# Moving the one-pass matmul operands of a two-branch kernel to the low part of SBUF

## The chip, the core and the metric

The kernel runs on one core of a Trainium2 chip. The metric is the time of one execution on the device in microseconds: the median of several runs of the kernel. Beside the timed runs there is one profiled execution, from which the span (first to last instruction) and every trace row come.

## The reference

Two independent branches are computed, and their results stand side by side in the output of 2048 rows and 2048 columns.

```python
# branch A: attention with 32 query heads of width 32 and one shared key/value head
q = (x @ wq).reshape(B, S, H, Dh)          # S = 2048, D = 1024, H = 32, Dh = 32
k = x @ wk; v = x @ wv
p = softmax(einsum("bhqd,bkd->bhqk", q, k) * Dh ** -0.5)
a = einsum("bhqk,bkd->bhqd", p, v).reshape(B, S, H * Dh) @ wo
# branch B: real part of a Fourier transform along the hidden and the sequence axis
re = einsum("bsd,ed->bse", xb, dft_hid_re); im = einsum("bsd,ed->bse", xb, dft_hid_im)
y = einsum("ts,bse->bte", dft_seq_re, re) - einsum("ts,bse->bte", dft_seq_im, im)
out = concatenate([a, y], axis=-1)
```

All inputs are float32.

## The kernel before, in words

**Precision.** A float32 matmul in full precision shows in the trace as two matmul records. A matmul whose two operands are of type float32r shows as one, here called a one-pass matmul. A float32 value is split into a rounded part and a remainder (names ending in h and l, "hi" and "lo"), and a product of full accuracy is made of three one-pass matmuls, hi·hi, hi·lo and lo·hi (`product`, line 373). The scores also use one-pass matmuls: key and query are stacked on the partition axis as (kh, kh, kl) against (qh, ql, qh), so that one pass makes the three terms. The attention weights times v (`pv`, line 821) use full float32.

**Streams of work.** TensorE carries two interleaved streams.

- The attention goes by 32 units of one block of 512 queries and one group of four heads. Each unit has 32 steps. `scores(s)` (line 744) makes two one-pass matmuls into a PSUM tile `pss` with moving operand `kst` and weights from `qst`; VectorE takes a negated maximum from it, and ScalarE an exponential and its sum (`row_sums`), out of which come the softmax constants. `expo(n)` (line 807), 44 steps behind, makes the transposed scores: two one-pass matmuls into `pst` with moving operand `qst` and weights from `kst`, and ScalarE writes their exponential to `p`. Three times in a unit `pv` multiplies `p` with `v` in full float32, four heads at a time. 
- Everything else is a queue of groups: the projection of the queries, the products of the Fourier branch and of the output projection (block recursions with seven products for eight). Each group adds up products of a left item (weights, tiles `mh` and `ml`) and a right item (moving operand, tiles `rh` and `rl`) into a PSUM tile `psb`. `take(n)` (line 379) issues n of these matmuls; `level` (line 933) spreads them over the steps of the attention, so that a step has about five. In a step in which `pv` runs, `level` issues none.

The order on each engine is the order of the program: every instruction goes through a wrapper that keeps it (line 79 is the line of that wrapper, and so the line that every instruction shows in the profile).

**How the items come.** For both lines of items (`Line`, line 154) SyncE loads raw blocks to staging tiles (`r0`, `r1` for the right, `m0`, `m1` for the left), GpSimd adds or subtracts them where a recursion asks for it, rounds them to `rh` or `mh` and writes the remainder to `rl` or `ml` (`hi_r`, `hi_m`, `lo`). 14 buffers of `rh` and of `rl` and four of `mh` and of `ml` go round.

**The end.** After the last unit the last eight groups run without scores between them. Their last right item meets the newest attention output, tiles `oh` and `ol`, as weights (`last_block`, line 364), while the moving operand is `rh` or `rl`.

**Where the tiles lie.** SBUF tiles come from pools. A pool takes its place when it is opened, from the left (low addresses upwards) by default, or from the right (high addresses downwards) with `side="right"`. Before the change:

- from the left, in this order: `keep` (`kst`, `v`, the identity), `qsp` (three tiles of `qst`, 8 KB in a partition each), `pp` (13 tiles of `p`, 4 KB each), `sm` (maxima, sums and the softmax constants), `onp` (`rb`, `ov`, `oh`, `ol`, 2 KB each);
- from the right, in this order: `r0p` and `m0p` (staging, five tiles of 2 KB each), `rp` (28 tiles of 2 KB), `mp` (8 tiles of 2 KB), `yp` (6 tiles of 2 KB), `op` (3 tiles of 2 KB).

The two stacks together nearly fill the partition. All pools live as long as the kernel, so no two of them ever share a place. At the start, before `p`, `rb` and the staging tiles have their own use, they hold the blocks of the attention input.

Of the kernel before, what the change touches and what calls it, by code (L numbers as in the profile page):

```python
# [101 lines left out]
def tile_kernel(ctx: ExitStack, tc, xT, wq, wkv, wo, xbT, wT, cT, out):  # L102
# [8 lines left out]
    def pool(stack, name, bufs, **kw):  # L111
        kw.setdefault("reuse_waits", "tile")
        return stack.enter_context(tc.tile_pool(name=name, bufs=bufs, **kw))
# [28 lines left out]
    NR, NM = 14, 4  # L142
    r0p = pool(ctx, "r0p", NR0, side="right")
    m0p = pool(ctx, "m0p", NM0, side="right")
    rp = pool(ctx, "rp", NR, side="right")
    mp = pool(ctx, "mp", NM, side="right")
    yp = pool(ctx, "yp", NY, side="right")
    op = pool(ctx, "op", 3, side="right")

# [566 lines left out]
    qsp = pool(ctx, "qsp", 1)  # L716
    rows = []
    NP = 13
    pp = pool(ctx, "pp", NP)
    sm = pool(ctx, "sm", 2)  # L720
    onp = pool(ctx, "onp", 1)

    units = [(b, g) for b in range(NQ) for g in range(NG)]
    SU = 32
# [308 lines left out]
```

## Time and profile before

| | |
|---|---|
| runs (three) | 2742.67 us median, 2741.53 to 2744.46 |
| profiled execution, span | 2740.7 us; no time around the span is recorded for it |
| TensorE (PE) busy | 2733.4 us, 13820 matmuls |
| weight loads (PEld) busy | 1917.8 us, 13820 |
| VectorE (DVE) busy | 1596.6 us |
| ScalarE (ACT) busy | 2159.8 us |
| GpSimd (POOL) busy | 1721.8 us |
| TensorE clock granted | 1.000 of full speed on average |

A row of the groups reads: line, engine, operation, out<-in by tile names, shapes, xcount, then busy time in us and the mean length of one in ns, then the idle time of the engine before them and what ended it. In `MATMUL psb<-rh,mh`, the first name behind the arrow is the moving operand and the second the weights. A row of the timeline begins with the start and the length in us; rows of one kind behind each other are merged, with their count at the end (x2). Matmul lengths overlap the next matmul and their ends are modelled, so the time that one takes of TensorE is read from one start to the next.

### The profile page before, as it was taken

To read this page: it belongs to the slowest core of one execution; us is meant where nothing else is said; L and a number is where in the kernel's file an instruction comes from. 1 tells how busy PE (TensorE), PEld (TensorE's weight loads), DVE (VectorE), ACT (ScalarE), POOL (GpSimd) and SP (SyncE) were. 2 spreads that over 40 slices of the span, in tenths; PEclk is the share of its full clock that TensorE was granted. 3 is DMA by queue.
4 is the path that set the end of the run, shared out by engine and by line. 5 is a ranking of instruction groups with operands and counts; after the bars stand their busy time and mean duration, and the time that the engine had idled before them with its cause. 6 is when DMAs were issued, how large, how long until landed. Compare 5 with 4: busy or idle time off the path is not lost.

```text
span 2740.7 us, 40561 instructions
## 1 busy us (share of the span) xinstructions
PE 2733.4 (100%) x13820; PEld 1917.8 (70%) x13820; DVE 1596.6 (58%) x1826; ACT 2159.8 (79%) x3131; POOL 1721.8 (63%) x1711
## 2 busy tenths in 40 slices
PE   9999999999999999999999999999999999999999
PEld 6876767667676767667676776667676676767667
DVE  5766666666676666555565556666555555655411
ACT  3588878888887888888888888888888888888741
POOL 4854425777647558765556665576787887865751
PEclk9999999999999999999999999999999999999999
DMA  8643336887777666564354688874675765644565
GB/s 273 191 136 120 117 96 205 281 270 232 248 261 271 202 219 187 168 203 136 125 158 149 184 251 285 290 253 124 209 222 158 219 192 160 206 137 136 185 208 188
DMA packets 316931, 538.24 MB, mean 196 GB/s; under 512 B 35962, under 2 KB 63354, under 8 KB 316666
## 3 DMA queue, kind: packets, MB, share of 16 engines
q1 hardware_dynamic: 315572, 533.69, 61.6%
q8 instruction: 109, 1.79, 0.3%
q10 hardware_dynamic: 1152, 1.97, 0.2%
q14 instruction: 98, 0.80, 0.1%
HBM read 395.58 MB, written 138.15 MB: 195 GB/s over the span
## 4 chain that ended last, share of the span: by engine, by line
PE 98%; DMA 1%; SPq 0%; issue 0%; POOL 0%; ACT 0%; DVE 0%; DVEq 0%; POOLq 0%; ACTq 0%
PE psb L79 61%; PE pss L79 19%; PE pst L79 18%; DMA y<-u 0%; SPq L79 0%; DMA y<-c 0%; DMA qh<-in_wo_dram 0%; DMA rb<-r 0%; DMA m<-in_wq_dram 0%; POOL rl L79 0%; ACT p L79 0%; DVE y L79 0%; POOL ml L79 0%; DVE nm L79 0%; POOL m L79 0%
## 5 line engine op out<-in xcount | busy, mean ns | idle before, releaser
L79 DVE TENSOR_REDUCE nm<-pss 128x1 f32<-128x1024 f32 x1024 | 1252.8, 1224 | 572.5 <-PE pss L79 571.0
L79 ACT ACTIVATE p<-pst 128x1024 f32<-128x1024 f32 x1026 | 1056.0, 1029 | 449.7 <-PE pst L79 445.9
L79 ACT ACTIVATE pss<-pss,nm 128x1024 f32<-128x1024 f32 x1024 | 1116.0, 1090 | 61.3 <-DVE nm L79 59.2
L79 PE MATMUL psb<-rh,mh 128*128 128x512 f32 x1790 | 705.4, 394 | 1.0 <-DVE y L79 0.9
L79 PE MATMUL psb<-rh,ml 128*128 128x512 f32 x1790 | 704.2, 393 | 0.0
L79 PE MATMUL psb<-rl,mh 128*128 128x512 f32 x1790 | 704.0, 393 | 0.0
L79 PE MATMUL pss<-kst,qst 128*128 128x512 f32 x2048 | 653.7, 400 | 0.3
L79 PE MATMUL pst<-qst,kst 128*128 128x512 f32 x2048 | 650.3, 398 | 0.8 <-ACT p L79 0.7
L79 POOL TENSOR_TENSOR ml<-m,mh 128x512 fp32r<-128x512 f32 x366 | 471.8, 1289 | 35.8 <-ACT mh L79 26.5
L79 PEld LDWEIGHTS pss<-kst,qst 128*128 128x128 f32 x2048 | 374.6, 188 | 160.9 <-issue 76.3
L79 PE MATMUL psb<-p,v 128*32 128x512 f32 x4096 | 459.3, 594 | 0.0
L79 PEld LDWEIGHTS pst<-qst,kst 128*128 128x128 f32 x2048 | 374.9, 188 | 110.1 <-ACT p L79 26.1
L79 PEld LDWEIGHTS psb<-rh,mh 128*128 128x128 f32 x1790 | 336.2, 188 | 85.7 <-issue 2.4
L79 PEld LDWEIGHTS psb<-rl,mh 128*128 128x128 f32 x1790 | 336.1, 188 | 79.8 <-DVE rl L79 1.2
L79 PEld LDWEIGHTS psb<-rh,ml 128*128 128x128 f32 x1790 | 336.2, 188 | 79.0
L79 POOL CAST mh<-m 128x512 fp32r<-128x512 f32 x365 | 223.0, 611 | 245.9 <-PE psb L79 218.7
L79 PEld LDWEIGHTS psb<-p,v 128*32 128x32 f32 x4096 | 123.3, 110 | 283.7 <-issue 275.8
L79 POOL TENSOR_TENSOR m<-m,m 128x512 f32<-128x512 f32 x220 | 283.4, 1288 | 58.1 <-DMA m<-o 23.2
L79 POOL TENSOR_TENSOR rl<-r,rh 128x512 fp32r<-128x512 f32 x208 | 268.2, 1290 | 4.0
L79 POOL CAST rh<-r 128x512 fp32r<-128x512 f32 x208 | 127.5, 613 | 199.9 <-PE psb L79 149.6
L79 ACT ACTIVATION_READ_ACCUMULATOR pss<-pss,nm 128x1 f32 x1024 | 212.5, 207 | 0.0
L79 POOL TENSOR_TENSOR r<-r,r 128x512 f32<-128x512 f32 x120 | 154.8, 1290 | 72.8 <-DMA r<-in_wT_dram 44.8
(92 smaller groups left out, 790.5 us busy)
## 6 DMA issues: line engine op xcount, KB each, us to landing
m<-in_cT_dram SPq DMA_DIRECT2D x384, 256.0 KB
r<-s SPq DMA_DIRECT2D x192, 256.0 KB
y<-y SPq DMA_DIRECT2D x128, 256.0 KB
r<-in_wT_dram SPq DMA_DIRECT2D x88, 256.0 KB
m<-in_xbT_dram SPq DMA_DIRECT2D x88, 256.0 KB
y<-u SPq DMA_DIRECT2D x80, 256.0 KB
m<-in_wq_dram SPq DMA_DIRECT2D x64, 256.0 KB
qst<-qh SPq DMA_DIRECT2D x64, 256.0 KB
```

Source lines behind the costliest of these rows:

```text
L79: return lambda *a, **k: self.tc.keep_in_program_order(f(*a, **k))
```

## The change

Five pools change sides. `rp` and `mp`, which hold the operands of the products, move from the right to the left stack and come to lie right above `keep`, below `qsp`. `pp`, `sm` and `onp` move from the left to the right stack, below `op`. The pools keep their sizes and the number of their buffers, and everything else of the kernel is as before.

```diff
     r0p = pool(ctx, "r0p", NR0, side="right")
     m0p = pool(ctx, "m0p", NM0, side="right")
-    rp = pool(ctx, "rp", NR, side="right")
-    mp = pool(ctx, "mp", NM, side="right")
+    rp = pool(ctx, "rp", NR)
+    mp = pool(ctx, "mp", NM)
     yp = pool(ctx, "yp", NY, side="right")
     op = pool(ctx, "op", 3, side="right")
...
     qsp = pool(ctx, "qsp", 1)
     rows = []
     NP = 13
-    pp = pool(ctx, "pp", NP)
-    sm = pool(ctx, "sm", 2)
-    onp = pool(ctx, "onp", 1)
+    pp = pool(ctx, "pp", NP, side="right")
+    sm = pool(ctx, "sm", 2, side="right")
+    onp = pool(ctx, "onp", 1, side="right")
```

## The prediction

> **What bounds the kernel now.** I read the page from the top first: busy shares, the clock, then the chain that ended last.
>
> ```profile
> span 2740.7 us, 40561 instructions
> PE 2733.4 (100%) x13820; PEld 1917.8 (70%) x13820; DVE 1596.6 (58%) x1826; ACT 2159.8 (79%) x3131; POOL 1721.8 (63%) x1711
> PEclk9999999999999999999999999999999999999999
> PE 98%; DMA 1%; SPq 0%; issue 0%; POOL 0%; ACT 0%; DVE 0%; DVEq 0%; POOLq 0%; ACTq 0%
> ```
>
> TensorE is busy for 2733.4 of 2740.7 us at full clock, and 98% of the chain is TensorE. Only the time between the starts of two matmuls can move the end. The groups by form tell how many there are, and which other engine is nearest.
>
> ```profile
> L79 PE MATMUL psb<-rh,mh 128*128 128x512 f32 x1790 | 705.4, 394 | 1.0 <-DVE y L79 0.9 <-ACT rh L79 0.2
> L79 PE MATMUL pss<-kst,qst 128*128 128x512 f32 x2048 | 653.7, 400 | 0.3
> L79 PE MATMUL pst<-qst,kst 128*128 128x512 f32 x2048 | 650.3, 398 | 0.8 <-ACT p L79 0.7
> L79 PE MATMUL psb<-p,v 128*32 128x512 f32 x4096 | 459.3, 594 | 0.0
> L79 PEld LDWEIGHTS pst<-qst,kst 128*128 128x128 f32 x2048 | 374.9, 188 | 110.1 <-ACT p L79 26.1 <-issue 3.4
> ```
>
> The 400 ns are a modelled length with overlap; what counts is start to start. One-pass matmuls are three times 1790 products, 2048 + 2048 of the scores, and some 150 in other PSUM tiles at the end: about 9620. So I went to the timeline of TensorE: one step of the main loop, and the starts of the steps behind it.
>
> ```profile
> 1500.21 0.63 PE L79 MATMUL pss<-kst,qst 128*128 128x512 f32 x2
> 1500.68 0.63 PE L79 MATMUL pst<-qst,kst 128*128 128x512 f32 x2
> 1501.15 0.40 PE L79 MATMUL psb<-rh,mh 128*128 128x512 f32 x1
> 1501.38 0.39 PE L79 MATMUL psb<-rl,mh 128*128 128x512 f32 x1
> ...
> 1502.06 0.40 PE L79 MATMUL psb<-rl,mh 128*128 128x512 f32 x1
> 1502.30 0.63 PE L79 MATMUL pss<-kst,qst 128*128 128x512 f32 x2
> ...
> 2458.72 0.62 PE L79 MATMUL pst<-qst,kst 128*128 128x512 f32 x2
> ...
> 2481.67 0.62 PE L79 MATMUL pst<-qst,kst 128*128 128x512 f32 x2
> ```
>
> A step is two score matmuls, two of the transposed scores and five products: nine in 2.09 us. Between the last two rows lie eleven such steps: 22.95 us, 2.086 a step, 0.2318 a matmul. Now the end of the kernel, where products run alone and then meet the weights of the last unit (oh, ol).
>
> ```profile
> 2711.95 0.40 PE L79 MATMUL psb<-rh,ml 128*128 128x512 f32 x1
> 2712.18 0.39 PE L79 MATMUL pss<-rh,oh 128*128 128x512 f32 x1
> 2712.41 0.39 PE L79 MATMUL pss<-rl,oh 128*128 128x512 f32 x1
> ...
> 2714.74 0.40 PE L79 MATMUL psb<-rh,ol 128*128 128x512 f32 x1
> 2714.98 0.39 PE L79 MATMUL psb<-rh,mh 128*128 128x512 f32 x1
> 2715.21 0.39 PE L79 MATMUL psb<-rl,mh 128*128 128x512 f32 x1
> 2715.43 0.39 PE L79 MATMUL psb<-rh,ml 128*128 128x512 f32 x1
> ...
> 2719.06 0.39 PE L79 MATMUL psb<-rh,mh 128*128 128x512 f32 x1
> ```
>
> From 2715.43 to 2719.06 lie sixteen products: 3.63 us, 0.2267 each, the settled pitch. The twelve with oh or ol as weights take 2.80 us, 0.2333 each. Their moving operands are still rh and rl; only the place of the weights is another, and the next products settle again within two or three.
>
> The places follow from the pools. Counted in bytes within a partition, the left pools hold kst from 17,024, qst from 27,264 to 51,839, p to 105,087, oh and ol from 111,872 to 115,967. The right ones hold mh from 135,136, ml to 151,519, rh and rl from 151,520 to 208,863. So products read both operands high, scores read both low, and the oh matmuls read weights low and moving data high. Within the high part the place doesn't matter: the sixteen settled products walk through several of the 28 buffers of rh and rl and several columns of mh and ml. My reading: a matmul whose weights and moving data lie in different parts is late, and it takes some matmuls to settle afterwards. A loop step crosses twice, from products to scores and back. It takes 2.086 us where nine settled ones would take 9 x 0.2267 = 2.040: 46 ns more.
>
> **The change part by part.** No instruction is added, removed or reordered, no wait changes, and every DMA has its size and queue. Only addresses change. Summing the pool sizes in the new order, rh and rl come to 27,264 to 84,607, mh and ml to 100,991, qst to 125,567; kst stays. p, the sums and exponentials go high with the staging, oh and ol to about 130,400.
>
> *One-pass matmuls.* All operands of a loop step then lie in one stretch, below 125,568, as the products' did before within 73,700 bytes. I take the settled pitch for all nine. There are 1024 steps (2048 pst matmuls by two). 96 of them hold the p,v matmuls (three for each of 32 units) and no product, so they don't cross; some 31 hold a transpose that upsets the pitch anyway, for which I take half. The other 1024 - 96 - 31 = 897 x 46 ns give 41.3 us, and 31 x 23 ns give 0.7. The prologue has 44 score steps of two score matmuls and seven products:
>
> ```profile
> 92.89 0.62 PE L79 MATMUL pss<-kst,qst 128*128 128x512 f32 x2
> 94.98 0.62 PE L79 MATMUL pss<-kst,qst 128*128 128x512 f32 x2
> ```
>
> Nine in 2.09 us here too: 44 x 46 ns = 2.0 us. Bounds: nothing from below (the pitch of the low part by itself is never seen settled, since runs there are four long); from above everything that TensorE takes beyond 9620 x 0.2267 = 2181 us. Its busy time less 459.3 of p,v and some 23 of other full-precision matmuls and transposes is 2251, so 70 us; the part beyond 44 is starts after the p,v blocks and waits, which no address removes.
>
> *p,v matmuls* now read p high and v low, a crossing. The nearest rows are the full-precision matmuls that make k and v, whose weights lie low (ov, 110 kB up) and whose moving data alternate:
>
> ```profile
> 28.55 0.59 PE L79 MATMUL pss<-p,ov 128*64 128x512 f32 x1
> 28.56 0.59 PE L79 MATMUL pss<-r,ov 128*64 128x512 f32 x1
> 28.98 0.59 PE L79 MATMUL pss<-p,ov 128*64 128x512 f32 x1
> 29.41 0.59 PE L79 MATMUL pss<-p,ov 128*64 128x512 f32 x1
> ```
>
> p lies low, r high, and each pair takes 0.43 us whichever comes first. I take 0; at the other end 7 ns (0.2333 less 0.2267) on each of the 1024 groups of four, 7 us.
>
> *Other engines.* POOL multiplies low tiles and combines high ones in the same time:
>
> ```profile
> L79 POOL TENSOR_TENSOR r<-r,r 128x512 f32<-128x512 f32 x120 | 154.8, 1290 | 72.8 <-DMA r<-in_wT_dram 44.8 <-DMA r<-s 12.7 <-DMA s<-y 12.2
> L79 POOL TENSOR_TENSOR oh<-ov,rb 128x512 f32<-128x512 f32 x16 | 20.7, 1293 | 112.9 <-DVE ov L79 109.3 <-DMA ql<-y 3.6
> ```
>
> 1290 against 1293 ns: place costs it nothing, and I take the same for DVE and ACT, with 63, 58 and 79% busy as cover.
>
> *What is late next.* ACT. Where it is behind, its cycle from p to p is 1.99 us:
>
> ```profile
> 1379.05 1.03 ACT L79 ACTIVATE p<-pst 128x1024 f32<-128x1024 f32 x1
> 1381.04 1.04 ACT L79 ACTIVATE p<-pst 128x1024 f32<-128x1024 f32 x1
> ```
>
> A step of nine at 2.04 still covers that, by 0.05 instead of 0.10. A step of eight does not, and where they come every other step TensorE already waits for p:
>
> ```profile
> 238.72 0.63 PE L79 MATMUL pst<-qst,kst 128*128 128x512 f32 x2
> ...
> 1380.32 0.62 PE L79 MATMUL pst<-qst,kst 128*128 128x512 f32 x2
> 1382.18 0.68 PE L79 MATMUL pst<-qst,kst 128*128 128x512 f32 x2
> 1384.32 0.62 PE L79 MATMUL pst<-qst,kst 128*128 128x512 f32 x2
> ...
> 2679.04 0.39 PE L79 MATMUL pst<-qst,kst 128*128 128x512 f32 x1
> ```
>
> Eight from 1380.32 to 1382.18 (1.86 us), then nine in 2.14: together 4.00, ACT's pace. Such pairs gain nothing. Waits of this kind add up to 26.1 us before the weight loads of pst, most of it hidden by the matmul ahead. Of the plain steps I count 89 of eight (the first starts at 238.72, the last at 2679.04), so with their partners some 178, and put 130 of them at ACT's pace: 130 x 46 ns = 6.0 us lost (0 if the slack that TensorE has on ACT after each p,v block covers them, 8.2 if all are caught).
>
> The sum: 41.3 + 0.7 + 2.0 - 6.0 = 38.0 us less. The profiled span of 2740.7 becomes 2702.7; the median of the runs, 2742.67, lies 2.0 us above that span, so the time is 2704.7.
>
> One rule speaks against all this. The Trainium skill, "SBUF — State Buffer", section "Who interferes with whom", gives TensorE two read ports, one for the moving operand and one for the weights, independent of each other, says that it never waits on anyone, and makes nothing depend on the place within a partition. By that rule the time stays 2742.7; the twelve matmuls at 0.2333 beside the sixteen at 0.2267 disagree with it, and they are all that disagrees.
>
> **The rivals.**
> *Nothing moves (2742.7).* The late pitch could come from something else that the scores and the oh matmuls share and the settled products lack: a change of the tile pair by itself, or the semaphores that free pss and pst. For it: the scores among themselves, all low, don't run settled (1500.21 to 1501.15 is 0.235 each), although they share one part. Against it: four are too few to settle, and PSUM banks change at the end of the kernel too, between products, at the settled pitch.
>
> *Slower.* The cost may belong to weights read from the low part, whatever the moving data. For it: all low weights that are seen, of scores and of oh, run at 0.233 to 0.235. Against it: the products behind the crossing, whose weights are high, start late too (1501.15 to 1501.38 is 0.23). Then each of the nine takes 0.2333, a step 2.100 us, 14 ns more than 2.086, on 941 steps 13 us, and some 400 products outside such steps 2.6 us more: 2742.7 + 16 = 2759. It decides from the point where the settled pitch of the low part is over 0.232.
>
> *Half.* The part that counts may end inside the new block (between rl and qst, say), as no trace shows a pair across 52,000 to 110,000. Then about one crossing of two stays: half of 38.0, about 2724.
>
> Whether it is the part, or the 32 bytes by which right-hand tiles stand off a multiple of 64 while left-hand ones don't, the trace can't tell; the change makes both alike, so the sum is the same.
>
> **How the numbers follow.** Like operands settle: 0.64, and its own range is 2697 to 2714 (all 44 us of steps and no loss to ACT give 2699; p,v matmuls that do feel the crossing and ACT's full loss give 2714; 2 us for the runs' spread at the lower end). Half: 0.09. Nothing: 0.15. Slower: 0.12. A change of 0.2%, 5.5 us, is about what can be told from none here. The first two are faster (0.73), the third the same, the fourth slower. The range runs from 2692 to 2746: it takes in nothing-moves with the spread of the runs and leaves out the slower case and little else.
>
> **What would show it.** Right: a nine-matmul step of 2.04 us from pss to pss, ten in 2.27, the score matmuls at 0.227 among products, and the p,v groups unchanged; ACT's busy time the same with a larger share, and more idle time behind ACT p in the weight loads of pst. The prologue's step falls alike, with no ACT p in it. Wrong: a step still at 2.09 (the cause is in the pair or the semaphores), one at 2.10 or more (low weights), or steps at 2.04 with a span that doesn't follow, which would mean new waits on ACT, POOL or the loads that feed rh and mh.

## The result and the profile after

The changed kernel takes 2709.98 us (median, 2709.76 to 2710.24) against 2742.1 us in the same runs: the ratio is 0.988, with a 95% interval of 0.9866 to 0.9894. The profiled execution has a span of 2708.2 us in a time of 2709.95; it was 32.5 us longer before. The granted clock of TensorE is 1.0 in both. The forecast was 2704.7.

From the page of the changed kernel, the rows that answer to those of before:

```profile
span 2708.2 us, 40561 instructions
PE 2700.9 (100%) x13820; PEld 1917.0 (71%) x13820; DVE 1595.7 (59%) x1826; ACT 2135.1 (79%) x3131; POOL 1721.4 (64%) x1711
PE 99%; DMA 0%; ACT 0%; DVE 0%; POOL 0%; issue 0%; SPq 0%; ACTq 0%; DVEq 0%; POOLq 0%
```

The instructions are the same in number. The busy time of TensorE fell by 32.5 us, the whole difference of the spans; VectorE and GpSimd are unchanged within 1 us. ScalarE's busy time fell by 24.7 us, although the mean lengths of its three large groups are the same within 2 ns (1091 after 1090, 1031 after 1030, 209 after 207): its records overlap more, they did not get shorter. From the groups by form:

```profile
L79 PE MATMUL psb<-p,v 128*32 128x512 f32 x4096 | 459.3, 594 | 0.0
L79 PEld LDWEIGHTS pst<-qst,kst 128*128 128x128 f32 x2048 | 373.5, 188 | 107.4 <-ACT p L79 30.8 <-issue 3.4
```

The p,v matmuls take 459.3 us as before. The waits for ACT's p grew from 26.1 to 30.8 us. The timeline of TensorE, one step of nine in the main loop, and two starts of the prologue:

```profile
92.12 0.61 PE L79 MATMUL pss<-kst,qst 128*128 128x512 f32 x2
94.16 0.61 PE L79 MATMUL pss<-kst,qst 128*128 128x512 f32 x2
...
2442.15 0.62 PE L79 MATMUL pss<-kst,qst 128*128 128x512 f32 x2
2442.60 0.61 PE L79 MATMUL pst<-qst,kst 128*128 128x512 f32 x2
...
2444.19 0.39 PE L79 MATMUL pss<-kst,qst 128*128 128x512 f32 x1
```

Nine matmuls take 2.04 us in both places, 0.2267 each, where they took 2.09. Two score matmuls now take 0.45 us instead of 0.47. So the gain came where the forecast put it. Why it came had still to be found out, since two readings gave the same number: the part of the partition, and the offset of the tiles.

### The profile page after: what moved, and what is told of

It reads as the page before. It is cut to its first block, busy times and chain, and to the rows that moved or that the text cites. A ratio compares the mean times of both kernels' runs of the same rounds, so it can differ in the third digit from the quotient of the medians.

```text
span 2708.2 us, 40561 instructions
## 1 busy us (share of the span) xinstructions
PE 2700.9 (100%) x13820; PEld 1917.0 (71%) x13820; DVE 1595.7 (59%) x1826; ACT 2135.1 (79%) x3131; POOL 1721.4 (64%) x1711
## 4 chain that ended last, share of the span: by engine, by line
PE 99%; DMA 0%; ACT 0%; DVE 0%; POOL 0%; issue 0%; SPq 0%; ACTq 0%; DVEq 0%; POOLq 0%
PE psb L79 62%; PE pss L79 19%; PE pst L79 18%; DMA y<-c 0%; ACT pss L79 0%; DVE nm L79 0%; DMA rb<-r 0%; DMA m<-in_wq_dram 0%; SPq L79 0%; ACT p L79 0%; DVE y L79 0%; POOL ml L79 0%; POOL m L79 0%; DVE qh L79 0%; ACT mh L79 0%
## 5 line engine op out<-in xcount | busy, mean ns | idle before, releaser
L79 ACT ACTIVATE p<-pst 128x1024 f32<-128x1024 f32 x1026 | 1056.3, 1030 | 443.6 <-PE pst L79 432.1
L79 ACT ACTIVATE pss<-pss,nm 128x1024 f32<-128x1024 f32 x1024 | 1117.3, 1091 | 59.5 <-DVE nm L79 56.9
L79 PE MATMUL pss<-kst,qst 128*128 128x512 f32 x2048 | 645.3, 396 | 0.3
L79 PE MATMUL pst<-qst,kst 128*128 128x512 f32 x2048 | 642.9, 395 | 0.6 <-ACT p L79 0.4
L79 PE MATMUL psb<-p,v 128*32 128x512 f32 x4096 | 459.3, 594 | 0.0
L79 PEld LDWEIGHTS pst<-qst,kst 128*128 128x128 f32 x2048 | 373.5, 188 | 107.4 <-ACT p L79 30.8
```

The costliest lines, as they stand in the source:

```text
L79: return lambda *a, **k: self.tc.keep_in_program_order(f(*a, **k))
```

## The experiments

The theory on record was that of the part: late where weights and moving data lie on different sides of a border. Its rivals were the offset of tiles against each other, and weights read from the low part being slow in themselves.

**A map of places.** A kernel of its own, with nothing at work but TensorE:

```diff
+    def run(m, mo, w, wo_):
+        o = ps[n[0] % 2]
+        n[0] += 1
+        for _ in range(REP):
+            te.matmul(o, s[w][:, wo_:wo_ + P], s[m][:, mo:mo + W], start=True, stop=True)
```

> This kernel leaves the whole computation out: it fills SBUF with 25 tiles of 8 KB a partition (sa at 16,512 to sy at 213,120, all on multiples of 64 bytes) and runs blocks of 40 one-pass matmuls, 128x512, with the weights in one tile and the moving data in another, no other engine at work. First weights in sc (32,896), moving data in each tile in turn; then weights in su (180,352); then the same with the moving data fixed and the weights going round; then one pair with its moving data shifted by 4 to 400 bytes; then weights in steps of 512 bytes across 131,072. Theory of the part: 0.2267 us per matmul where both lie on one side of a border between 115,968 and 135,136, and about 0.233 where they lie on different sides, in both directions; no effect of the shifts. Theory of the 32 bytes: 0.2267 for all pairs of tiles, about 0.233 where the moving data are shifted by 32 bytes. Theory of low weights: 0.233 for all blocks with weights in the low tiles, 0.2267 for all with high ones, wherever the moving data lie.

Timeline of this kernel; each row is a block of 40 (`REP`) matmuls of the same pair, and the time to the next block's start over 40 is the pitch. Moving tile and weights tile stand behind the arrow (one name where they are the same tile).

```profile
34.11 9.23 PE L31 MATMUL pb<-sd,sc 128*128 128x512 f32 x40
43.17 9.23 PE L31 MATMUL pa<-se,sc 128*128 128x512 f32 x40
...
188.24 9.23 PE L31 MATMUL pa<-su,sc 128*128 128x512 f32 x40
197.31 9.23 PE L31 MATMUL pb<-sv,sc 128*128 128x512 f32 x40
...
251.71 9.23 PE L31 MATMUL pb<-sc,su 128*128 128x512 f32 x40
260.77 9.23 PE L31 MATMUL pa<-sd,su 128*128 128x512 f32 x40
...
922.64 9.62 PE L31 MATMUL pb<-sc 128*128 128x512 f32 x40
932.11 9.49 PE L31 MATMUL pa<-sc 128*128 128x512 f32 x40
...
950.70 9.49 PE L31 MATMUL pa<-sc 128*128 128x512 f32 x40
960.03 9.31 PE L31 MATMUL pb<-sc 128*128 128x512 f32 x40
...
1134.66 9.47 PE L31 MATMUL pa<-sc,sn 128*128 128x512 f32 x40
1143.96 9.26 PE L31 MATMUL pb<-sc,so 128*128 128x512 f32 x40
```

Weights low and moving data low (34.11 to 43.17) take 9.06 us; weights low and moving data at 180,352 (188.24) take 9.07; weights at 180,352 and moving data low (251.71) take 9.06: 0.2267 a matmul each, but for the rounding of the rows. Of the 100 blocks of the four sweeps 99 read like these; the first, at the very start of the kernel, takes 10.78 us. So the theory of the part fell, and that of low weights with it. A moving operand shifted by 4 bytes takes 0.2368 (922.64 to 932.11), by 32 bytes 0.2333 (950.70 to 960.03). The last pair belongs to the steps towards 131,072: there the weights were moved by 128 bytes modulo 256, still below that address, and took 0.2325, while the steps of 2,048 and 512 bytes before it were settled, and so was the tile above after its first matmuls. That block told that the offset modulo 256 was the thing to vary.

**32 bytes of padding, all operands low (e2).** The changed kernel with a pad of 32 bytes below the product tiles and one above:

```diff
+    off_a = pool(ctx, "off_a", 1).tile([P, 8], F32, name="off_a")
     rp = pool(ctx, "rp", NR)
     mp = pool(ctx, "mp", NM)
+    off_b = pool(ctx, "off_b", 1).tile([P, 8], F32, name="off_b")
+    gp.memset(off_a, 0.0)
+    gp.memset(off_b, 0.0)
```

> The changed kernel with rh, rl, mh and ml 32 bytes further up, so that they stand 32 bytes off a multiple of 64 as before the change, while kst and qst stand on multiples of 64 as before; all of them stay low. Theory of the part: 2710 us as changed, steps of nine at 2.04. Theory of the 32 bytes: the crossings are back, steps of nine at 2.086, about 2742.

2741.84 us; ratio to the kernel before 0.9999 (0.9989 to 1.0008). The whole gain is gone with every operand still low. From its timeline, eleven steps of nine:

```profile
2461.22 0.63 PE L79 MATMUL pst<-qst,kst 128*128 128x512 f32 x2
...
2484.21 0.63 PE L79 MATMUL pst<-qst,kst 128*128 128x512 f32 x2
```

22.99 us, 2.090 a step. It does not show 32 bytes by itself, though: the second pad put qst at 192 modulo 256 bytes, with kst at 128 and the products at 160, so that the scores were a mismatched pair too.

**Weights of the products high again (e3).**

```diff
-    mp = pool(ctx, "mp", NM)
+    mp = pool(ctx, "mp", NM, side="right")
```

> The changed kernel with mh and ml back in the high part (192,480 to 208,863), rh and rl low, kst and qst low. Every product then reads weights high and moving data low, the scores both low. Theory of the part: the products never settle, five at 0.233 and four score matmuls that don't settle among them, a step of nine at 2.09 to 2.10, and the products alone at the end at 0.233 too: 2745 to 2760 us, slower than the changed kernel and no faster than the kernel before. Theory of low weights: products at 0.2267, since their weights are high, scores late: 2720 to 2745.

2744.47 us, 1.0007 of before (0.9997 to 1.0016): as the theory of the part had it but for half a microsecond below its range. It agrees with the offset as well, since mh and ml came to 224 modulo 256 and rh and rl stayed at 128. The products alone at its end:

```profile
2703.22 0.40 PE L79 MATMUL pst<-rh,mh 128*128 128x512 f32 x1
...
2708.14 0.40 PE L79 MATMUL psb<-rh,mh 128*128 128x512 f32 x1
```

From the first of these rows to the last lie 21 products, 4.92 us, 0.2343 each: a mismatched pair stays late for good. This run could not tell the two theories apart; the map did.

**A map of offsets.**

> This kernel too leaves the whole computation out; it runs blocks of 40 one-pass matmuls, and only the offset of the moving data to the weights changes. Section a: moving data 0, 16, 32 up to 256 bytes further up, one tile after the other (sa to sq). Section b: weights 32 to 256 bytes further up (sr to sy). Section c: both further up by 4, 8, 16, 32, 64, 96 and 128 bytes. Sections d and e: five matmuls of one pair and four of another in turn, the second pair further up by 96 bytes in d and by 256 in e. Theory of the relative offset (the settled pitch holds where moving data and weights stand at the same place modulo 256 bytes): in a and b 0.2267 at 0 and 256 bytes alone and 0.229 to 0.237 between; all of c at 0.2267; d at about 0.2318, as in the loop of the kernel before, and e at 0.2267. Theory of the absolute place (tiles have to stand on a multiple of 64 or 128 bytes): c late at 4 to 32 bytes, d settled or nearly so.

```profile
24.05 9.50 PE L31 MATMUL pa<-sc 128*128 128x512 f32 x40
33.39 9.49 PE L31 MATMUL pa<-sd 128*128 128x512 f32 x40
42.72 9.33 PE L31 MATMUL pa<-se 128*128 128x512 f32 x40
51.88 9.41 PE L31 MATMUL pa<-sf 128*128 128x512 f32 x40
...
144.99 9.24 PE L31 MATMUL pa<-sp 128*128 128x512 f32 x40
154.06 9.28 PE L31 MATMUL pa<-sq 128*128 128x512 f32 x40
163.17 9.49 PE L31 MATMUL pb<-sr 128*128 128x512 f32 x40
...
209.81 9.33 PE L31 MATMUL pb<-sw 128*128 128x512 f32 x40
218.99 9.49 PE L31 MATMUL pb<-sx 128*128 128x512 f32 x40
...
228.31 9.24 PE L31 MATMUL pb<-sy 128*128 128x512 f32 x40
237.39 9.66 PE L31 MATMUL pc<-sa 128*128 128x512 f32 x40
246.89 9.40 PE L31 MATMUL pc<-sb 128*128 128x512 f32 x40
256.13 9.48 PE L31 MATMUL pc<-sc 128*128 128x512 f32 x40
265.45 9.28 PE L31 MATMUL pc<-sd 128*128 128x512 f32 x40
274.56 9.26 PE L31 MATMUL pc<-se 128*128 128x512 f32 x40
...
301.86 1.30 PE L31 MATMUL pd<-sa 128*128 128x512 f32 x5
303.00 1.10 PE L31 MATMUL pd<-sb 128*128 128x512 f32 x4
303.94 1.31 PE L31 MATMUL pd<-sa 128*128 128x512 f32 x5
...
347.58 1.30 PE L31 MATMUL pe<-sa 128*128 128x512 f32 x5
...
349.62 1.30 PE L31 MATMUL pe<-sa 128*128 128x512 f32 x5
```

Moving data 32 bytes up (sc, 24.05) take 0.2335, 64 bytes (se) 0.2290, 256 bytes (sq) 0.2267 but for the first matmuls of the block. Weights 256 bytes up (sy) are settled, weights 32 bytes up (sr) are not, and weights 192 bytes up (sw), which is 64 short of 256, take 0.2295, about as much as moving data 64 bytes up: it is the place of the one against the other, modulo 256. Four blocks don't fit that theory. Moving data 240 bytes up, 16 short of 256, are settled as well (sp, 144.99 to 154.06). And the pair that is shifted together settles by 32 bytes and more (sd, 265.45 to 274.56, but for its first matmuls), but not by 4, 8 or 16 bytes (sa, sb and sc of section c: 0.2375, 0.2310 and 0.2330). So in these blocks a match was enough only where both started on a multiple of 32. Section d is the loop of the kernel before in small: five of one pair and four of another 96 bytes off take 2.08 us (301.86 to 303.94), where the loop took 2.086. In section e, 256 bytes off, nine took 2.04 (347.58 to 349.62), although the pair of tiles changes just as often.

**The kernel before, aligned (e5).** All pools on their old sides, and 96 bytes above the right-hand stack:

```diff
+    off = pool(ctx, "off", 1, side="right").tile([P, 24], F32, name="off")
+    gp.memset(off, 0.0)
     r0p = pool(ctx, "r0p", NR0, side="right")
```

> The kernel before with every pool where it was, and 96 bytes left free above the right-hand stack, so that rh, rl, mh and ml stand at 128 modulo 256 bytes as kst and qst do, products still high and scores low. Theory of the relative offset: the whole gain without moving a pool, steps of nine at 2.04, 2710 us within 2. Theory of the part: nothing, 2742.

2710.77 us, 0.9883 of before (0.9868 to 0.9897): the whole gain, with products high and scores low.

```profile
1501.88 0.61 PE L79 MATMUL pss<-kst,qst 128*128 128x512 f32 x2
1503.92 0.61 PE L79 MATMUL pss<-kst,qst 128*128 128x512 f32 x2
```

The step of nine is 2.04 us. This run decides it: that the operands came to lie low did nothing.

**The step between the pairs alone, and 256 bytes.** As in e2, but with qst moved by 256 bytes (e6); and rh, rl, mh, ml and qst all moved by 256 (e7).

> The changed kernel with rh, rl, mh and ml 32 bytes further up and qst 256, so that the pairs within the products and within the scores keep the same place modulo 256 bytes and only the step between the two kinds is off by 32. Theory of the relative offset: two crossings a step as before the change, steps of nine at 2.08 to 2.09, 2735 to 2745 us. If crossings cost nothing and only pairs count: 2710.

> The changed kernel with rh, rl, mh, ml and qst 256 bytes further up, and nothing else. Theory of the relative offset modulo 256 bytes: as the changed kernel, 2710 us within 2. If the place of the one-pass operands to each other counts in bytes and not modulo 256: late, over 2720.

e6 takes 2733.26 us (ratio 0.9964, 0.9951 to 0.9977), e7 2710.06 (0.9882, 0.9866 to 0.9899). So crossings cost by themselves, though 2 us less than the lower end expected; 256 bytes cost nothing. Eleven steps of e6:

```profile
2450.90 0.62 PE L79 MATMUL pst<-qst,kst 128*128 128x512 f32 x2
...
2473.71 0.62 PE L79 MATMUL pst<-qst,kst 128*128 128x512 f32 x2
```

22.81 us, 2.074 a step: 34 ns over 2.040, where 96 bytes cost 46. The price of a crossing differs between these two offsets.

**Where the rest of the forecast went.** First ScalarE made lighter (e4), then the steps made even, on the changed kernel (e8, with the changed kernel beside it, e9) and on the kernel before (e10). The edit of e4:

```diff
+        dve.memset(nm[u][:, 8:10], 1.0)
...
-        act.activation(ps, ps, AF.Exp, bias=nm[u][:, j, i:i + 1], accum_out=nm[u][:, 8 + j, i:i + 1])
+        act.activation(ps, ps, AF.Exp, bias=nm[u][:, j, i:i + 1])
```

> The changed kernel without the sums of the first exponentials (no accumulator is read on ScalarE, a constant stands in their place), which leaves the softmax sums out. ScalarE's cycle falls by about 0.1 us. Theory that ScalarE's pace took what was missing of the forecast gain: steps of eight at 1.81 instead of 1.87 on average and no wait before pst, 7 to 9 us less than the changed kernel: 2701 to 2703. Theory that the rest is lost to the late pitch behind the p,v blocks: 2708 to 2710.

The edit of e8 and e10:

```diff
+    AHEAD = 60
...
-        take(round(left / more))
+        take(max(round(left / more), 5 if goal(n + more) + AHEAD > pos["fill"] else 0))
```

> The changed kernel with the products spread so that no step of the attention gets fewer than five of them as long as the queue is less than 60 ahead of its plan: hardly any step of eight one-pass matmuls is left while scores run, and steps of ten become fewer. The sum of products is the same. Theory that ScalarE's pace of 1.99 us behind steps of eight took the missing part, with the late pitch that each such wait leaves behind it: plain steps at 2.04 nearly everywhere, 6 to 12 us less than the changed kernel, 2698 to 2704. If waits on ScalarE are made up elsewhere in any case: 2708 to 2712.

> The changed kernel once more, beside the one with even steps: 2710 us within 1.

> The kernel before (nothing moved) with the same even steps as in e8. If the waits on ScalarE that e8 removed were all made by the change, steps of nine at 2.086 cover ScalarE's 1.99 and this gains nothing: 2742. If they were there before, this gains as much as e8 did on the changed kernel, 10 us: 2733. Between the two, what it gains less than e8 is what the change gave back to ScalarE: I expect 4 to 7 us here, 2736 to 2739.

e4 takes 2703.77 us (0.9857, 0.9843 to 0.9872), 6 less than the changed kernel and 0.8 over the range that was expected. e8 takes 2700.11 us (0.9845, 0.9832 to 0.9859), and the changed kernel beside it 2709.88 (0.988, 0.9866 to 0.9893): even steps are worth 9.8 us there. On the kernel before (e10) they are worth 4.4 us: 2738.51 against 2742.88 (0.9985, 0.9976 to 0.9994). So 5.4 us of the gain had gone into uneven steps; that it is ScalarE's pace that takes it there is shown by e4, which keeps the steps uneven and makes only ScalarE lighter. The weight loads of pst in e4, e8 and e10, one row of each kernel's groups:

```profile
L79 PEld LDWEIGHTS pst<-qst,kst 128*128 128x128 f32 x2048 | 375.4, 188 | 101.0 <-ACT p L79 24.2 <-issue 3.4
```

```profile
L79 PEld LDWEIGHTS pst<-qst,kst 128*128 128x128 f32 x2048 | 378.6, 188 | 96.5 <-ACT p L79 15.6 <-issue 3.4
```

```profile
L79 PEld LDWEIGHTS pst<-qst,kst 128*128 128x128 f32 x2048 | 380.1, 188 | 101.5 <-ACT p L79 11.5 <-issue 3.4
```

From 30.8 us in the changed kernel to 15.6 with even steps: half of the waits for p stood behind uneven steps. On the kernel before they fell by about as much (26.1 to 11.5), where even steps are worth less than half: this idle time is not the time lost. The version with matched offsets and even steps is the fastest complete kernel of this study, 42.9 us under the kernel before.

## Why the prediction was right, and where it wasn't

The time lies 5.3 us above the forecast and inside its own range of 2697 to 2714. Point by point:

- *The step of nine.* Forecast 2.04 us, measured 2.04, in the prologue too. Right.
- *The reason named for it.* Wrong. The step that failed is the reading that a matmul "whose weights and moving data lie in different parts" is late. The rows were read rightly (0.2333 with oh as weights, 0.2267 beside it), but place and offset differed together in them: modulo 256 bytes the products stood at 224, the scores at 128, oh and ol at 0. The sentence that the trace can't tell the two apart was right, and it put the offset at 32 bytes of 64, where it is the match modulo 256. The number survived because the new order of the pools brought rh, rl, mh, ml, kst and qst all to 128 modulo 256. (oh and ol came to 96, and their matmuls still take 0.233 each in the changed kernel.) This was luck of the pool sizes: e2 has the same places but for 32 and 64 bytes, and gains nothing.
- *The rival "half"* assumed a border inside the low block. The map shows no border. *"Slower"* had the low weights cost by themselves; low weights took 0.2267. *"Nothing moves"* is refuted by the result, and the reason that it gave, the change of the tile pair by itself, by section e of the map of offsets. The rule of the Trainium skill in "SBUF — State Buffer", section "Who interferes with whom", ties nothing to the place, and the map agrees: 99 blocks at one pitch. That the two reads are independent doesn't fit the maps: the pitch goes from 0.2267 to 0.2368 with the offset of the one to the other alone.
- *p,v matmuls and other engines at nothing.* Right: 459.3 us before and after, POOL 1721.8 and 1721.4. The sign "ACT's busy time the same" was off by 24.7 us, though its instructions kept their lengths. The reading that the steps with p,v hold no product was wrong: 54 of the 95 in the trace hold one to five. It changed little, as these 95 steps gained 0.8 us together.
- *ACT is late next, 6.0 us lost.* Right in kind and about right in size: 5.4 us by e8 and e10, 7.2 us by the count of steps in the next point, inside the 8.2 that the prediction gave as the most. The short steps are seen in the timeline of the changed kernel, starts of pst:

```profile
881.21 0.63 PE L79 MATMUL pst<-qst,kst 128*128 128x512 f32 x2
883.30 0.62 PE L79 MATMUL pst<-qst,kst 128*128 128x512 f32 x2
885.34 0.62 PE L79 MATMUL pst<-qst,kst 128*128 128x512 f32 x2
...
895.54 0.62 PE L79 MATMUL pst<-qst,kst 128*128 128x512 f32 x2
897.35 0.71 PE L79 MATMUL pst<-qst,kst 128*128 128x512 f32 x2
899.51 0.45 PE L79 MATMUL pst<-qst,kst 128*128 128x512 f32 x1
```

  Eight from 895.54 in 1.81 us, as an unhindered step should, then nine in 2.16: the matmul waits for p, and the eight behind it start late until the pitch settles. Together 3.97, ACT's pace.
- *The term that was too large* is 897 plain steps x 46 ns = 41.3 us, with all crossings gone. Both traces hold the same steps in the same order, so each step can be set against itself, from its start of pst to the next. The 897 plain steps gained 29.8 us. Of the 11.5 us that are missing, 7.2 are missing on the 160 steps with eight matmuls or fewer and the steps of nine right behind them, which gained next to nothing; this is the loss to ACT that the sum had at 6.0, and in e4, with ScalarE lighter, these same steps take 4.6 us less than in the changed kernel. Another 2.0 are missing on the 64 steps right behind a p,v block, which gained 15 ns each and not 46: the one at 881.21 still takes 2.09 us, as the pitch has to settle after full-precision matmuls whether or not anything crosses. The sum had no term for that. The rest, some 2.3 us, is spread over the other steps. With 1.6 us in the prologue, where the sum had 2.0, 0.8 in the p,v steps and 0.3 in those with a transpose, the 29.8 make the 32.5 us between the two spans. With even steps in both kernels the move is worth 2738.51 - 2700.11 = 38.4 us, against the 44.0 that the sum had before ACT's share.

## What to carry to other kernels

Before a layout is changed for its place, look at the addresses modulo 256 bytes: weights and moving data of float32r matmuls that follow each other should match there and start on multiples of 32, as far as these shapes and offsets show it, and a pad of 96 bytes did here what moving five pools did. In the timeline a mismatch between two pairs shows as a start-to-start time that settles in long runs of one pair and rises wherever the other comes in; a mismatch within a pair shows as a time that never settles. When the steps of TensorE get shorter, here from 2.086 to 2.04 us, spread its work so that no step falls below the next engine's cycle; here that was worth another 9.8 us.

## What the runs showed of the hardware that was not expected

- A 128x512 float32r matmul with 128x128 weights, one after the other, takes 0.2267 us where moving data and weights match modulo 256 bytes, and 0.229 to 0.235 in the maps where they don't (0.2368 with the moving data 4 bytes off), wherever they lay between 16,512 and 221,311 bytes of the partition; 240 bytes of offset are an exception and settle. A match is not enough by itself: both shifted together by 4 bytes took 0.2375.
- The full-precision p,v matmuls don't feel it: moving p from 128 to 224 modulo 256 left their group at 459.3 us, and four of them at 0.429 us from start to start.
- After a wait or a block of another kind, the pitch takes some matmuls to settle even where all offsets match: in the step of the changed kernel at 897.35 one matmul starts 0.09 us late, and the eight starts behind it add another 0.03.
- What in the two reads makes the offset matter was not found; the runs show the dependence and no cause.
